# Which DMA queue carries the output stores: SyncE's or GpSimd's, in a fused attention and mixture kernel

## The chip, the cores and the metric

The kernel runs on one NeuronCore of a Trainium2 chip. The metric is the time of one execution on the device in microseconds (us). The core has TensorE (PE), VectorE (DVE), ScalarE (ACT), GpSimd (POOL) and SyncE (SP). Transfers between HBM and SBUF, the memory on the core, run on 16 DMA engines. An engine's sequencer issues a transfer to a queue. SyncE's transfers appear in the profile as queue q1 (hardware_dynamic), GpSimd's as queue q0 (software_dynamic). A transfer is moved as packets; the profile counts packets and bytes for each queue.

## The reference, cut to what matters

```python
# attention: q, k, v are (4, 8, 768, 64); half of the heads see all earlier keys,
# the others the first 4 keys and a window of 64
a = softmax(mask(q @ k.T / 8)); attn = a @ v
x = attn.transpose(0, 2, 1, 3).reshape(3072, 512)
# soft mixture of experts: 8 experts, 4 slots each, F = 1024
logits = x @ phi                                  # 3072 x 32
slot_input = softmax(logits, over rows).T @ x     # 32 x 512
slot_out[e] = relu(slot_input[e] @ w1[e]) @ w2[e] # 8 experts, 512 -> 1024 -> 512
out = softmax(logits, over slots) @ slot_out      # 3072 x 512, float32
```

The output is 3072 x 512 float32, 6.29 MB. It depends on all of `slot_out`, which depends on the last expert weight, so nothing can be stored before the end of the program.

## The kernel before, in words

The attention part works through 16 pairs of batch and heads and fills most of the time. During it GpSimd issues the loads of q, k, v and of the expert weights; its queue converts float32 in HBM to bf16 in SBUF on the way ("casting queue"). The loads follow each other on q0 without a pause. The order of all work is made at build time by a small planner (`Plan`): each piece of work (`pl.op`) has an engine, a key, costs and the work that it depends on; the planner places what can start earliest, the lower key first, and the instructions of each engine are emitted in that order.

The end of the program is what the change touches:

- The second weights of the last two experts are loaded in two column halves each (`load_half`), in the order 14.0, 15.0, 14.1, 15.1. With the first halves, columns 0 to 255 of `slot_out` can be finished (`SO.0`), with the second halves columns 256 to 511 (`SO.1`).
- The 3072 rows of the output are 6 row groups `gi` of 512 rows. Row 512 * gi + 4 * p + r lies on partition p, at place r (0 to 3). So one partition of a group holds 4 whole rows, 8 KB, one after another both in SBUF (`ot_view(gi)`) and in HBM.
- `out_tile` makes one tile (gi, r): a matmul on PE (line 1130) into a PSUM bank, then a scaled copy to SBUF on DVE (line 1140) or ACT (line 1138).
- Groups 0 to 2 (`NL = 12` tiles) are made in two halves: first the "l" tiles (left, columns 0 to 255, after `SO.0`), later the "r" tiles (right, columns 256 to 511, after `SO.1`). Groups 3 to 5 are made whole ("f" tiles, 512 columns).
- `store(eng, m, gi, r0, r1, cs, key)` (issue at line 1149) stores the places r0 to r1 - 1 of a group, columns `cs`, through GpSimd's queue if `eng` is "POOL", otherwise through SyncE's. It depends on the copies of just those tiles. A store of half rows has runs of 1 KB in HBM, which lie 2 KB apart; a store of whole rows has 8 KB on each partition in one piece. Nothing is converted in a store: SBUF and HBM are both float32.

The stores before: on GpSimd the left ones of group 0 (place 0: 128 KB; places 1 to 3: 384 KB); on SyncE the left ones of groups 1 and 2 in two of 256 KB each, the right ones of groups 0 to 2 in two of 256 KB each, and the whole rows of groups 3, 4 and 5, 1024 KB each. That is 2 stores on GpSimd and 13 on SyncE, which also issues three loads at the start. GpSimd has no other work in this part. At the program's end SyncE waits for every store to land, and all engines meet in barriers (line 1217).

Of the kernel before, what the change touches and what calls it, by code (L numbers as in the profile page):

```python
# [226 lines left out]
def kernel(  # L227
# [101 lines left out]
    def on(eng, occ, late=0.18):  # L329
        return {eng: (occ, occ + late)}  # L330
# [651 lines left out]
    kt = T * 16 + 10  # L982
# [137 lines left out]
    def ot_view(gi):  # L1120
        return slots[wbuf[gi].slot][:, 0:8 * KB].bitcast(F32).rearrange("p (r d) -> p r d", r=4)
# [3 lines left out]
    def out_tile(m, gi, r, c0, c1, key):  # L1125
        bf, w = Buf("BK"), 256 * (c1 - c0)
        cs = slice(256 * c0, 256 * c1)

        def emit_om(o):
            nc.tensor.matmul(banks[bf.slot][:, 0:w], out_lhs(gi, r), slot_out[:, cs], start=True, stop=True)  # L1130

        a = pl.op(f"OM.{gi}.{r}.{c0}", on("PE", 0.06 + w / 2400.0, 0.27), key, deps=so_e[c0:c1], acq=[bf],
                  emit=emit_om, mode="full", mm=1)

        def emit_oe(o):
            d, sc_ = ot_view(gi)[:, r, cs], rrow[:, 4 * gi + r:4 * gi + r + 1]
            if o.eng == "ACT":
                nc.scalar.activation(d, banks[bf.slot][:, 0:w], ACT.Copy, scale=sc_)  # L1138
            else:
                nc.vector.tensor_scalar(d, banks[bf.slot][:, 0:w], sc_, None, op0=ALU.mult)  # L1140

        x, y = (0.24 + w / 1070.0, 0.13 + w / 960.0)
        oe[m, gi, r] = pl.op(f"OE.{gi}.{r}.{c0}", {"ACT": (x, x + 0.19), "DVE": (y, y + 0.17)}, key, deps=[a, o_rw[gi]],
                             rel=[bf], emit=emit_oe)

    def store(eng, m, gi, r0, r1, cs, key):
        def emit_st(o):
            dst = out[512 * gi:512 * (gi + 1), :].rearrange("(p r) d -> p r d", r=4)
            (nc.gpsimd if eng == "POOL" else nc.sync).dma_start(dst[:, r0:r1, cs], ot_view(gi)[:, r0:r1, cs])

        pl.op(f"ST.{m}.{gi}.{r0}", on(eng, 0.7), key, deps=[oe[m, gi, r] for r in range(r0, r1)], emit=emit_st)

    NL = 12
    halved = [(gi, min(4, NL - 4 * gi)) for gi in range((NL + 3) // 4)]
    for gi, n in halved:
        for r in range(n):
            out_tile("l", gi, r, 0, 1, kt + 30 + 0.1 * (4 * gi + r))
    for gi, r0, r1 in [(0, 0, 1), (0, 1, 4)] + [(gi, x, x + 2) for gi, n in halved[1:] for x in (0, 2)]:
        store("SP" if gi else "POOL", "l", gi, r0, r1, slice(0, 256), kt + 31 + gi + 0.1 * r0)
    for gi, n in halved:  # L1160
        for r in range(n):
            out_tile("r", gi, r, 1, 2, kt + 40 + 0.1 * (4 * gi + r))
        for r0, r1 in [(0, 2), (2, 4)]:
            store("SP", "r", gi, r0, r1, slice(256, 512), kt + 41 + gi + 0.1 * r0)
    for gi in range(6):
        n = dict(halved).get(gi, 0)
        for r in range(n, 4):
            out_tile("f", gi, r, 0, 2, kt + 41 + 0.1 * (4 * gi + r))
        if n < 4:
            store("SP", "f", gi, n, 4, slice(0, 512), kt + 42 + gi)  # L1170

    pl.limit = kt - 0.2
    pl.tune(SHIFTS)
# [48 lines left out]
```

## Time and profile before

| what | value |
|---|---|
| median of 3 runs | 147.64 us (147.49 to 147.65) |
| the profiled execution | 147.56 us |
| its span, first to last instruction | 145.8 us |
| DMA packets, bytes | 14648, 33.40 MB |
| queue q0 (GpSimd) | 26.22 MB, 92.9% of 16 engines' span |
| queue q1 (SyncE) | 6.88 MB, 12.7% |
| busy share of PE, DVE, ACT, POOL | 85%, 76%, 74%, 28% |

The profile is one execution. Its windows give for a stretch the busy time of each engine with the number of instructions, the clock that was granted to PE, the mean share of the 16 DMA engines that were busy, and the rate in GB/s of what they moved (a load that converts is counted by the bytes that it writes). A share above 1 means that packets overlap on an engine. The DMA view of a stretch gives the packets, the bytes and the share of each queue, and for an issue the time until its data landed.

### The profile page before, as it was taken

The page shows a single profiled execution, that of the slowest core. Times are in us where ns is not written, and L with a number is a line of the kernel's source. Part 1 is how long each engine was busy: PE and PEld are TensorE (multiplying, and loading weights), DVE is VectorE, ACT ScalarE, POOL GpSimd, SP SyncE. Part 2 cuts the span into 40 slices and gives each one's busy share as a digit, 9 for nine tenths or more (in the row PEclk, how much of TensorE's full clock was granted, in tenths as well). Part 3 has the DMA queues.
Part 4 walks back from the last instruction along what each step waited for, and adds up shares of the span by engine and source line. Part 5 has one row for each costly group of instructions (what it writes and reads, how often), then busy time and mean ns, then how long its engine had stood idle before and what let it go on. Part 6 is the DMA issues. An engine that isn't in the chain of part 4 may idle for free.

```text
span 145.8 us, 4941 instructions
## 1 busy us (share of the span) xinstructions
PE 124.6 (85%) x2134; PEld 82.3 (56%) x2134; DVE 110.8 (76%) x254; ACT 107.9 (74%) x147; POOL 40.5 (28%) x73
## 2 busy tenths in 40 slices
PE   6959989999999999999989999999959899869100
PEld 4437566676776758776548766666737355444000
DVE  1796399999999999999799899999983312449700
ACT  3152799999999988999998999999971461549300
POOL 6988631310311470100170011405380000110000
PEclk9985699999999999999999999999995999999965
DMA  5999999999999999999999999999999999999995
GB/s 135 277 208 211 215 215 214 212 216 214 215 214 214 216 215 214 216 214 211 215 214 215 214 216 219 212 217 215 217 210 215 211 194 197 185 321 362 407 420 247
DMA packets 14648, 33.40 MB, mean 229 GB/s; under 512 B 867, under 2 KB 7651, under 8 KB 14115
## 3 DMA queue, kind: packets, MB, share of 16 engines
q0 software_dynamic: 11184, 26.22, 92.9%
q1 hardware_dynamic: 3442, 6.88, 12.7%
q8 instruction: 16, 0.26, 0.6%
q14 instruction: 6, 0.04, 0.1%
HBM read 52.49 MB, written 6.29 MB: 403 GB/s over the span
## 4 chain that ended last, share of the span: by engine, by line
PE 28%; DVE 25%; DMA 18%; ACT 15%; issue 6%; POOL 1%; SPq 0%; DVEq 0%; ACTq 0%; POOLq 0%
DMA qk<-in_moe_w_dram 15%; ACT pt L735 11%; PE sc L665 6%; DVE pt L681 5%; PE pv L809 5%; DVE xv L833 5%; DMA phf<-in_moe_phi_dram 4%; DVE qk L336 3%; PE tr L613 3%; PE tr L639 3%; PE bk L1130 3%; PE tr L872 2%; DVE slot L1140 2%; DVE vf L714 2%; PE tr L845 2%
## 5 line engine op out<-in xcount | busy, mean ns | idle before, releaser
L735 ACT ACTIVATE pt<-sc 128x1024 bf16<-128x1024 f32 x80 | 77.0, 1049 | 3.0 <-PE sc L665 2.8
L665 PE MATMUL sc<-qk 64*128 64x512 bf16 (+3 forms) x256 | 31.3, 311 | 1.2 <-ACT pt L735 0.8
L681 DVE TENSOR_TENSOR pt<-pt,msk 128x1024 bf16<-128x1024 bf16 (+1 forms) x48 | 29.0, 609 | 2.0 <-ACT pt L735 1.8
L809 PEld LDWEIGHTS <-pt 128*128 128x128 bf16 x640 | 23.7, 98 | 6.2 <-issue 5.2
L809 PE MATMUL pv<-vx,pt 128*128 128x65 bf16 x320 | 25.9, 194 | 0.3 <-DVE xv L833 0.2
L809 PE MATMUL pv<-vf,pt 128*128 128x65 bf16 x320 | 21.6, 196 | 0.9 <-DVE xv L833 0.9
L347 POOL DMA_DIRECT2D slot<-in_moe_w_dram x11 | 7.8, 705 | 39.3 <-PE tr L639 29.5
L639 PE MATMUL tr<-ident,slot 128*64 128x128 bf16 (+1 forms) x448 | 16.3, 219 | 0.4 <-ACT qk L334 0.3
L336 DVE COPY qk<-tr 128x768 bf16<-128x768 bf16 (+2 forms) x33 | 15.1, 481 | 1.5 <-PE tr L613 1.3
L639 PEld LDWEIGHTS <-slot 128*64 128x64 bf16 (+1 forms) x448 | 13.1, 109 | 5.1 <-issue 4.8
L833 DVE TENSOR_TENSOR xv<-pv,rs 128x768 bf16<-128x768 f32 (+1 forms) x17 | 15.5, 910 | 0.6
L665 PEld LDWEIGHTS <-qk 64*128 64x128 bf16 x256 | 10.4, 94 | 9.6 <-issue 3.3
L1140 DVE TENSOR_SCALAR slot<-bk,rrow 128x256 f32<-128x256 f32 (+1 forms) x19 | 9.2, 561 | 2.2 <-PE bk L1130 2.2
L896 POOL COPY expT<-eT 128x192 bf16<-128x192 bf16 x12 | 7.4, 657 | 12.2 <-ACT eT L879 12.2
L336 DVE COPY xv<-tr 128x512 bf16<-128x512 bf16 (+2 forms) x20 | 7.9, 409 | 2.4 <-PE tr L613 2.2
L845 PE MATMUL tr<-ident,xv 128*128 128x128 bf16 x96 | 8.4, 224 | 1.3 <-DVE xv L833 0.9
L613 PE MATMUL tr<-ident_u,slot 96*64 96x96 bf16 x192 | 7.3, 238 | 1.9 <-DVE phi L553 1.4
L613 PEld LDWEIGHTS <-slot 96*64 96x64 bf16 x192 | 6.3, 133 | 4.5 <-issue 4.1
L336 DVE COPY xT<-tr 128x768 bf16<-128x768 bf16 (+1 forms) x14 | 7.5, 538 | 1.1 <-PE tr L845 1.1
L1138 ACT ACTIVATE slot<-bk,rrow 128x256 f32<-128x256 f32 (+1 forms) x17 | 7.7, 569 | 0.9 <-PE bk L1130 0.9
L699 PE MATMUL tr<-ident,xv 128*128 128x128 bf16 x96 | 8.1, 220 | 0.0
L845 PEld LDWEIGHTS <-xv 128*128 128x128 bf16 x96 | 6.0, 99 | 2.9 <-DVE xv L833 1.7
(123 smaller groups left out, 169.0 us busy)
## 6 DMA issues: line engine op xcount, KB each, us to landing
slot<-in_moe_w_dram POOLq DMA_DIRECT2D x10, 1024.0 KB, 24.5
out_dram<-slot SPq DMA_DIRECT2D x3, 1024.0 KB, 6.2
out_dram<-slot SPq DMA_DIRECT2D x10, 256.0 KB, 3.2
slot<-in_q_dram POOLq DMA_DIRECT2D x2, 768.0 KB, 19.4
slot<-in_k_dram POOLq DMA_DIRECT2D x2, 768.0 KB, 24.1
qk<-in_moe_w_dram SPq DMA_DIRECT2D x1, 1024.0 KB, 6.1
slot<-in_v_dram POOLq DMA_DIRECT2D x2, 512.0 KB, 21.3
qk<-in_moe_w_dram POOLq DMA_DIRECT2D x1, 1024.0 KB, 17.5
```

What stands on the lines that cost most here:

```text
L336: nc.vector.tensor_copy(dst, src)
L347: acq=[buf] if buf else [], lead=1.3, emit=lambda o: nc.gpsimd.dma_start(dst(), src))
L613: nc.tensor.transpose(t[64 * i:64 * (i + 1), :, :, s, :], rv[:, i, 8 * c + s, :], ident_u)
L639: nc.tensor.transpose(t[64 * i:64 * (i + 1), :, s, :], rv[:, i, 8 * c + s, :], ident[0:R, 0:R])
L665: nc.tensor.matmul(scb[sc.slot][:, i, c:c + 128 * nb], kk, qq.rearrange("p b c -> p (b c)"), start=True, stop=True)
L681: nc.vector.tensor_tensor(pT, pT, mh, op=ALU.mult)
L699: nc.tensor.transpose(t[:, 128 * j:128 * (j + 1)], vT[:, 6 * n + j, :], ident)
L735: nc.scalar.activation(pTs[PTb[b, n].slot][:, :, 512 * g:512 * (g + 1)], scb[sc.slot], ACT.Exp, scale=scale)
L809: nc.tensor.matmul(pvb[:, bk, c:c + 65], lt, rhs, start=(j == 0), stop=(j == i))
L833: nc.vector.tensor_tensor(xo, pvw[:, :, :, 0:64], r.rearrange("p i (j o) -> p i j o", o=1).to_broadcast([P, 2, i1 - i0, 64]), op=ALU.mult)
L845: nc.tensor.transpose(t[:, 128 * i:128 * (i + 1)], xv[:, i, 128 * n:128 * (n + 1)], ident)
L1140: nc.vector.tensor_scalar(d, banks[bf.slot][:, 0:w], sc_, None, op0=ALU.mult)
```

## The change

All left stores go through GpSimd's queue, those of groups 1 and 2 in one transfer of 512 KB each. Of the right ones, the two of group 0 and the first of group 1 stay on SyncE (`4 * gi + r0 < 6`); the second of group 1 goes to GpSimd, and group 2 becomes one transfer of 512 KB there. Of the whole rows, group 3 goes to GpSimd; groups 4 and 5 stay on SyncE. Together with its three loads at the start, SyncE then issues eight transfers; GpSimd issues 7 stores instead of 2. The tiles and their order are as before.

```diff
-    for gi, r0, r1 in [(0, 0, 1), (0, 1, 4)] + [(gi, x, x + 2) for gi, n in halved[1:] for x in (0, 2)]:
-        store("SP" if gi else "POOL", "l", gi, r0, r1, slice(0, 256), kt + 31 + gi + 0.1 * r0)
+    for gi, r0, r1 in [(0, 0, 1), (0, 1, 4)] + [(gi, 0, n) for gi, n in halved[1:]]:
+        store("POOL", "l", gi, r0, r1, slice(0, 256), kt + 31 + gi + 0.1 * r0)
     for gi, n in halved:
         for r in range(n):
             out_tile("r", gi, r, 1, 2, kt + 40 + 0.1 * (4 * gi + r))
-        for r0, r1 in [(0, 2), (2, 4)]:
-            store("SP", "r", gi, r0, r1, slice(256, 512), kt + 41 + gi + 0.1 * r0)
+        for r0, r1 in [(0, 2), (2, 4)] if gi < 2 else [(0, n)]:
+            store("SP" if 4 * gi + r0 < 6 else "POOL", "r", gi, r0, r1, slice(256, 512), kt + 41 + gi + 0.1 * r0)
     for gi in range(6):
         n = dict(halved).get(gi, 0)
         for r in range(n, 4):
             out_tile("f", gi, r, 0, 2, kt + 41 + 0.1 * (4 * gi + r))
         if n < 4:
-            store("SP", "f", gi, n, 4, slice(0, 512), kt + 42 + gi)
+            store("SP" if gi > 3 else "POOL", "f", gi, n, 4, slice(0, 512), kt + 42 + gi)
```

## The prediction

> **What bounds the kernel now.** I read the page first (slices of the span), then the windows of the last 20 us, the DMA queues in narrow windows, and the timelines of GpSimd, SyncE, VectorE and ScalarE there.
>
> ```profile
> span 145.8 us, 4941 instructions
> DMA  5999999999999999999999999999999999999995
> ```
>
> The 16 DMA engines are at 90% or more in all slices but the first and the last. The stores are the end of that: the windows of the last 18 us show it against the engines.
>
> ```profile
> core 0: us, PE busy (x) PEld busy (x) DVE busy (x) ACT busy (x) POOL busy (x), PEclk, DMA share, GB/s
> 126.00:128.00 2.00, 1.94 (x20) 0.94 (x19) 2.00 (x6) 1.89 (x6) 1.12 (x2) 1.00 1.15 167
> 128.00:129.00 1.00, 0.52 (x6) 0.17 (x3) 0.44 (x2) 0.40 (x2) 0.22 (x1) 1.00 1.15 294
> 129.00:131.00 2.00, 1.35 (x26) 1.01 (x26) 0.49 (x2) 0.62 (x2) 0.00 (x0) 1.00 0.99 362
> 131.00:134.40 3.40, 3.37 (x19) 1.63 (x17) 3.40 (x9) 3.40 (x9) 0.00 (x0) 1.00 1.05 362
> 134.40:136.40 2.00, 0.86 (x3) 0.10 (x1) 2.00 (x4) 1.85 (x4) 0.00 (x0) 1.00 1.09 383
> 136.40:144.00 7.60, 0.00 (x0) 0.00 (x0) 1.13 (x2) 0.00 (x0) 0.00 (x0) 0.72 1.03 426
> ```
>
> The last two columns are the DMA share and rate. VectorE's last tile ends in the 136.4 window, yet transfers run on for 6 us at full share. From 129 on the share never falls below 0.99, so a tile that is ready earlier gains nothing; only bytes per microsecond count. And the rate is not constant: about 362 to 383 GB/s, then 426. The end hangs on the last store of SyncE:
>
> ```profile
> 137.60 0.36 SPq L1149 DMA_DIRECT2D out_dram<-slot  x1
> out_dram<-slot SPq DMA_DIRECT2D x1, 1024.0 KB, 7.3
> ```
>
> It lands at 137.60 + 7.3 = 144.9, and 0.9 us of closing barriers follow. The profiled execution took 147.56 us, 1.8 more than its span; the median of the runs is 147.64. I work from 147.56.
>
> Why the rate differs is seen in the DMA queues of three windows: 131.2 to 136.4 (only half-row stores on SyncE's queue, q1), 129.6 to 130.4 (GpSimd's 384 KB left store on q0, beside a little of q1), 138 to 143 (whole rows on q1).
>
> ```profile
> DMA packets 1991, 1.92 MB, mean 369 GB/s; under 512 B 119, under 2 KB 1991, under 8 KB 1991
> q1 hardware_dynamic: 1991, 1.92, 106.5%
> ...
> DMA packets 129, 0.32 MB, mean 406 GB/s; under 512 B 7, under 2 KB 64, under 8 KB 129
> q0 software_dynamic: 65, 0.27, 86.6%
> q1 hardware_dynamic: 64, 0.06, 20.8%
> ...
> DMA packets 292, 2.13 MB, mean 426 GB/s; under 512 B 32, under 2 KB 32, under 8 KB 32
> q1 hardware_dynamic: 292, 2.13, 101.3%
> ```
>
> A half row is 1 KB of HBM. SyncE's queue makes a packet of each (1.92 MB in 1991 packets); GpSimd's queue puts several in one (0.27 MB in 65 packets: 4 KB each), although the runs in memory are the same. Engine time per MB is share x 16 x window / MB: 1.065 x 16 x 5.2 / 1.92 = 46.1 for 1 KB packets, 0.866 x 16 x 0.8 / 0.27 = 41.1 for 4 KB, 1.013 x 16 x 5 / 2.13 = 38.1 for 8 KB.
>
> **The change part by part.** *What moves.* Left stores of row groups 1 and 2 (four of 256 KB become two of 512 KB), the second right store of group 1 (256 KB), the right ones of group 2 (two become one of 512 KB): 7 x 262144 B = 1.835 MB of half rows go from q1 to q0, that is from 1 KB to 4 KB packets. So does the first whole-row store (group 3, 1.049 MB), which has 8 KB packets already. SyncE keeps three right stores of 256 KB and two whole-row ones.
>
> *Packing.* 1.835 MB take 4.97 us at 369 GB/s and 4.52 at 406: 0.45 us gained. Bounds: at 426, the rate of 8 KB packets, 0.67 gained; at 358, which is the rate of a microsecond in which both queues were busy,
>
> ```profile
> DMA packets 222, 0.36 MB, mean 358 GB/s; under 512 B 22, under 2 KB 172, under 8 KB 222
> q0 software_dynamic: 59, 0.21, 55.5%
> q1 hardware_dynamic: 163, 0.15, 43.4%
> ```
>
> (129 to 130) it is 5.13, 0.15 lost. I take 406, because 0.27 of that window's 0.32 MB is just this kind of packet. [...]
>
> *The start.* The first left stores stand behind the last weight piece on q0. Before, SyncE's queue fills engines that are through with weights.
>
> ```profile
> 126.78 0.57 POOL L1149 DMA_DIRECT2D out_dram<-slot  x1 [17.83 <-DVE slot L1140]
> 127.46 0.76 POOL L1149 DMA_DIRECT2D out_dram<-slot  x1
> 127.35 2.03 SPq L1149 DMA_DIRECT2D out_dram<-slot  x4
> ...
> DMA packets 58, 0.03 MB, mean 99 GB/s; under 512 B 0, under 2 KB 58, under 8 KB 58
> DMA packets 29, 0.04 MB, mean 399 GB/s; under 512 B 0, under 2 KB 22, under 8 KB 29
> ...
> DMA packets 118, 0.09 MB, mean 299 GB/s; under 512 B 8, under 2 KB 116, under 8 KB 118
> q1 hardware_dynamic: 51, 0.05, 49.2%
> ```
>
> The windows are 127.6 to 127.9, 127.9 to 128.0 and 128.3 to 128.6. No 4 KB packet runs in the first, seven start in the second: GpSimd's first store needs 1.15 us from issue to first packet, so its second (127.46) runs from 128.6. SyncE's needs 0.95 (127.35 to 128.3). Between 128.3 and 128.6 q1 moved 0.05 MB that now has no carrier: 0.05 / 0.38 = 0.13 us lost. Bounds: 0 if the weights' remainder speeds up by as much, 0.26 if a second such stretch is lost.
>
> *The whole-row store on q0.* If q0 cuts it into 4 KB, 1.049 MB go from 426 to 406 GB/s: 0.12 lost; if it stays at 8 KB, 0. I take 0.06.
>
> *Issues and waits.* SyncE drops 8 of 13 issues, GpSimd gets 5 more of 0.57 to 0.76 us; it is idle (0.00 busy) after its second. Larger stores wait for four tiles instead of two. The queued bytes hide both, as long as they last, so I followed the supply. Left: the second store is through at about 129.6; the third is issued at 127.46 + 0.76 = 128.2 and has packets at 129.4, the fourth at about 130.2. After 128.6 there are 1.573 - 0.131 = 1.44 MB of left stores and by my estimate the time of 0.1 MB for the last weight packets; 1.54 / 0.406 = 3.8 us, to 132.4. The first right store:
>
> ```profile
> 129.46 0.40 PE L1055 MATMUL bk<-qk,xT 128*32 128x256 bf16 x8 [0.95 <-DMA qk<-in_moe_w_dram]
> 131.39 0.37 SPq L1149 DMA_DIRECT2D out_dram<-slot  x1
> 132.99 0.66 SPq L1149 DMA_DIRECT2D out_dram<-slot  x1
> 133.10 1.14 DVE L1140 TENSOR_SCALAR slot<-bk,rrow 128x256 f32<-128x256 f32 x2
> 135.12 0.57 SPq L1149 DMA_DIRECT2D out_dram<-slot  x1
> ```
>
> 131.39 + 0.95 = 132.35, in time by nothing; q1's left stores no longer run beside the last weight piece, whose landing starts this chain (129.46), so it may come 0.1 to 0.4 earlier. What packing gains on the left beyond that is lost as a gap. Right: SyncE's three need 0.786 / 0.369 = 2.1 us, to 134.5; GpSimd's first can be issued at 132.99 (packets 134.15), its second at about 133.6, when VectorE turns from half tiles to whole ones (134.75); both are through at 136.5. The whole-row store, issued by 135.12, has packets at 136.3. So no gap, with 0.2 us to spare. Sum: -0.45 + 0.13 + 0.06 = -0.26; 147.56 - 0.26 = 147.30.
>
> **The rivals.** *Packing saves nothing* where other traffic sets the pace. For: packets on q1 overlap (share 106.5%), so their price is less than engine time says, and the windows 129 to 131 show 362 with half of the bytes on q0. Against: 406 at 129.6 to 130.4. Then the start and the whole-row store remain: +0.13 + 0.06 = +0.19, 147.75. [...]
>
> *Slower: two queues beside each other cost the engines.* Before, both hold stores only from 128.3 to 131. Now they do from 134 on: 0.79 MB of half rows and 1.05 MB of whole rows on q0, against 0.3 and some 1.1 MB on q1. At the rates of one queue alone, 1.1 / 0.369 + 2.15 / 0.426 = 8.0 us for 3.25 MB; at the 358 of 129 to 130, 9.1. Against it -0.26 of the left part (1.049 MB) and +0.13 of the start: +0.9, 148.5. It decides from 398 GB/s down (8.03 + 0.13 us), and from 384 the kernel is slower by over 0.2%. Against: in 129 to 130 some engines were still short of stores (share 0.99, not 1.06).
>
> *Slower: GpSimd's drain ends last.*
>
> ```profile
> out_dram<-slot POOLq DMA_DIRECT2D x1, 384.0 KB, 4.1
> L1217 POOLq DRAIN  x3: 51/98/5717, 127.4 to 145.5; - x3
> ```
>
> Its first drain ran from 127.4 to 133.1, 1.6 us after its last store landed (127.46 + 4.1 = 131.5). If that follows the landing, a whole-row store on q0 that lands after 144.9 - 1.6 = 143.3 moves the end; landing with SyncE's last, by 1.6 - 0.26: 148.9. It is queued 2 us ahead of SyncE's last, so I hold this unlikely.
>
> **How the numbers follow.** About 0.2%, 0.3 us, is what a measurement of this kernel can tell from no change. The forecast, packing gains net between -0.7 and -0.1 us: 0.54, of which I give 0.42 to the part beyond 0.2% of the median (under 147.34). Nothing saved: 0.12. Two queues cost: 0.28, of which 0.04 stays within 0.2%. The drain: 0.06. So faster 0.42, same 0.12 + 0.12 + 0.04 = 0.28, slower 0.24 + 0.06 = 0.30. The likeliest is 147.3. The range goes from 146.9 (packing at its upper bound, -0.67, and a start that costs 0) to 148.2, most of the way to the second rival; the likeliest case alone has 147.0 to 147.5.
>
> **What would show it.** q0 gains 2.88 MB (26.22 to 29.1), q1 falls to 4.0. Right: about 400 GB/s in 129.5 to 132 with 4 KB packets on q0, share 1.0 or more to the end, and SyncE's last store landing at 144.6. Wrong: windows under 398 GB/s after 134 with both queues in them (the second rival), a DMA share under 0.95 around 132.4 or 136.4 (stores run out before tiles), more than 0.2 us lost before 129, or GpSimd's drain as the last to end.

## Result and profile after

The changed kernel took 148.25 us (median of 7 runs, 147.99 to 148.54) beside 147.65 us for the kernel before (7 runs, 147.49 to 147.79) on the same chip: ratio 1.0039, 95% interval 1.0025 to 1.0052. It is slower by 0.6 us, where 147.3 had been forecast. (All ratios here leave out executions in which the chip was disturbed, so they can differ a little from the quotient of medians.) The profiled execution took 148.25 us.

Of the page after, the span, the DMA slices and the queues:

```profile
span 146.5 us, 4933 instructions
DMA  4999999999999999999999999999999999999995
GB/s 132 285 210 211 214 215 216 214 215 216 210 214 216 214 213 215 215 214 215 214 214 214 215 215 215 215 216 215 215 215 215 207 195 198 178 337 346 376 418 242
q0 software_dynamic: 11840, 29.10, 97.6%
q1 hardware_dynamic: 1394, 4.00, 7.2%
```

The bytes moved as the change says: 29.10 MB on q0, 4.00 on q1. The slices of the span are too coarse to show the loss. The windows of the last 18 us, cut as those of the kernel before were (DMA share and GB/s are the last two columns):

```profile
126.00:128.00 2.00, 2.00 (x10) 1.19 (x8) 2.00 (x6) 2.00 (x5) 1.30 (x2) 0.50 1.08 168
128.00:129.00 1.00, 1.00 (x11) 0.25 (x10) 0.40 (x1) 0.60 (x2) 0.82 (x3) 0.76 0.96 219
129.00:131.00 2.00, 1.40 (x26) 1.05 (x26) 0.42 (x2) 0.56 (x2) 0.67 (x1) 1.00 0.97 359
131.00:134.40 3.40, 3.37 (x19) 1.63 (x18) 3.40 (x9) 3.40 (x8) 0.93 (x2) 1.00 1.00 352
134.40:136.40 2.00, 0.93 (x4) 0.15 (x2) 2.00 (x4) 1.92 (x4) 1.08 (x2) 1.00 0.94 337
136.40:144.00 7.60, 0.00 (x0) 0.00 (x0) 1.20 (x2) 0.00 (x0) 0.00 (x0) 0.65 1.01 411
```

Against before the rate is 294 to 219 in the window from 128, 362 to 359, 362 to 352, 383 to 337 and 426 to 411. Rate times length gives 0.08, 0.01, 0.03, 0.09 and 0.11 MB less, 0.32 MB in all; at 420 GB/s that is 0.76 us, and the span grew by 0.7. From 128 on no stretch is faster. The clock that was granted to TensorE was lower in this execution (0.50 in 126 to 128, 1.00 before), but the loss at the start is not its doing: the trace of e1 (below), with 1.00 there, has 232 GB/s in 128 to 129. Two things can lower a rate: engines that stand idle (share below 1) and packets that take longer (share at 1, low rate). Both are there, in the trace after:

```profile
129.60:130.00 0.40, 0.40 (x13) 0.19 (x13) 0.00 (x0) 0.02 (x1) 0.07 (x1) 1.00 0.79 287
134.80:135.20 0.40, 0.33 (x2) 0.00 (x0) 0.40 (x2) 0.40 (x2) 0.13 (x1) 1.00 0.86 310
135.60:136.00 0.40, 0.00 (x0) 0.00 (x0) 0.40 (x2) 0.40 (x2) 0.40 (x1) 1.00 0.66 236
137.20:137.60 0.40, 0.00 (x0) 0.00 (x0) 0.40 (x1) 0.00 (x0) 0.00 (x0) 1.00 0.92 338
```

In these four the engines ran dry; what is missing to a share of 1 is (0.21 + 0.14 + 0.34 + 0.08) x 0.4 = 0.31 us. The trace before has one such dip, too (0.85, 290 GB/s in 128.8 to 129.2), worth 0.06 us, so the change added 0.25 to 0.31 by this estimate. The timelines of GpSimd and SyncE tell whose stores were late:

```profile
126.57 3.10 POOL L1149 DMA_DIRECT2D out_dram<-slot  x4 [19.41 <-DVE slot L1140]
133.41 1.51 POOL L1149 DMA_DIRECT2D out_dram<-slot  x2 [3.74 <-DVE slot L1140]
135.53 0.55 POOL L1149 DMA_DIRECT2D out_dram<-slot  x1 [0.60 <-ACT slot L1138]
...
131.47 6.54 SPq L1149 DMA_DIRECT2D out_dram<-slot  x5
```

GpSimd issued its right stores from 133.41 and the whole-row one at 135.53; SyncE had issued the same two at 132.99 and 135.12 before. Longer packets show in the DMA queues of two windows in which q0 alone was at work, 130 to 131.2 (left store of group 1) and 131.6 to 132.8 (left store of group 2):

```profile
DMA packets 121, 0.47 MB, mean 389 GB/s; under 512 B 7, under 2 KB 7, under 8 KB 121
q0 software_dynamic: 121, 0.47, 99.6%
...
DMA packets 103, 0.40 MB, mean 336 GB/s; under 512 B 3, under 2 KB 5, under 8 KB 103
q0 software_dynamic: 101, 0.40, 95.6%
```

Both are packets of 4 KB on the same queue. Engine time per MB, worked out as in the prediction, is 0.996 x 16 x 1.2 / 0.47 = 40.7 for group 1, but 0.956 x 16 x 1.2 / 0.40 = 45.9 for group 2, about the 46.1 of 1 KB packets before.

### The profile page after: what moved, and what is told of

It reads as the page before. It is cut to its first block, busy times and chain, and to the rows that moved or that the text cites. A ratio compares the mean times of both kernels' runs of the same rounds, so it can differ in the third digit from the quotient of the medians.

```text
span 146.5 us, 4933 instructions
## 1 busy us (share of the span) xinstructions
PE 121.8 (83%) x2134; PEld 80.7 (55%) x2134; DVE 111.5 (76%) x254; ACT 108.3 (74%) x147; POOL 43.8 (30%) x78
## 3 DMA queue, kind: packets, MB, share of 16 engines
q0 software_dynamic: 11840, 29.10, 97.6%
## 4 chain that ended last, share of the span: by engine, by line
DVE 31%; PE 30%; DMA 16%; ACT 7%; issue 5%; POOL 3%; DVEq 0%; POOLq 0%; ACTq 0%
DMA qk<-in_moe_w_dram 16%; PE sc L665 7%; PE pv L809 7%; DVE pt L681 6%; DVE xv L833 5%; DVE qk L336 4%; ACT pt L735 4%; PE tr L639 4%; DVE xv L336 3%; PE bk L1130 3%; DVE vf L714 2%; PE tr L845 2%; PE tr L613 2%; PE tr L872 2%; DVE vx L336 2%
## 5 line engine op out<-in xcount | busy, mean ns | idle before, releaser
L1149 POOL DMA_DIRECT2D out_dram<-slot x7 | 4.8, 686 | 24.1 <-DVE slot L1140 23.2
L1130 PE MATMUL bk<-msk,expT 128*128 128x256 bf16 (+1 forms) x36 | 7.5, 355 | 0.9 <-ACT msk L1113 0.8
L613 PE MATMUL tr<-ident_u,slot 96*64 96x96 bf16 x192 | 5.8, 207 | 2.0 <-DVE phi L553 1.2
```

What stands on the lines that cost most here:

```text
L613: nc.tensor.transpose(t[64 * i:64 * (i + 1), :, :, s, :], rv[:, i, 8 * c + s, :], ident_u)
```

## Experiments

Theories, by the letters that the expectations use. A: GpSimd's stores come late and the engines run dry. B: 4 KB packets are no cheaper than 1 KB ones while VectorE and ScalarE write SBUF. C: two queues beside each other cost the engines. D: the rate falls with what is left in a queue. E: the rate depends on the place, that is on the address in SBUF where a group's data starts.

**The parts alone.** Each takes one part of the change and leaves the rest as before.

```diff
 e1_left_only    left, groups 1 and 2:  SP 4 x 256 KB  -> POOL 2 x 512 KB
 e2_right_only   right: group 1 second half -> POOL; group 2: SP 2 x 256 KB -> POOL 512 KB
 e3_whole_only   whole rows of group 3: SP -> POOL
```

> Only the left stores are as in the changed kernel (all on GpSimd, groups 1 and 2 in one transfer each); right and whole ones as before. Theory A (supply: GpSimd's stores reach the DMA engines later, so the engines run dry at the handovers): the start (0.06 MB less by 129.6 in the changed kernel's trace, 0.16 us) and the dip at 129.6 (294 GB/s, 0.05 us) stay, less some 0.05 us for 4 KB packets from 130 to 131: +0.1 to +0.2 us. Theory B (4 KB packets are not cheaper while VectorE and ScalarE write SBUF): the left part then loses only the start, +0.15. Prediction's view (packing gains 0.26 of the left part, start loses 0.13): -0.1. A and B are told apart in the trace: A wants dips in the rate, B packets of the same rate as 1 KB ones from 131.2 to 132.8.

> Only the right stores are as in the changed kernel (second of group 1 and all of group 2 on GpSimd); left and whole ones as before. Theory A: dips where SyncE's three right stores are through before GpSimd's first has packets (266 GB/s at 134.8 in the changed kernel) and before its second (291 at 135.6): +0.15 to +0.2 us. Theory B: 0.786 MB at about 345 instead of 383 GB/s: another +0.2 us, together +0.4. Prediction's view: -0.2 from packing.

> Only the whole rows of group 3 go through GpSimd's queue, all other stores as before. Theory A: SyncE's right stores keep the engines busy to about 136.9; GpSimd issues at about 135.5 and its packets come at about 137.0, so 0 to +0.15 us. Theory C (two queues beside each other cost the engines): 2.1 MB moved with both queues at work, at 358 instead of 426 GB/s up to +0.9 us; the changed kernel's trace at 427 GB/s there speaks for 0.

Measured: left alone 1.0013 [1.0001, 1.0025], right alone 1.0042 [1.0025, 1.0059], whole rows alone 1.0014 [0.9997, 1.0031]. No part gains. The right part costs most, and its own trace shows where:

```profile
134.40:134.80 0.40, 0.33 (x2) 0.00 (x0) 0.40 (x2) 0.40 (x2) 0.15 (x1) 1.00 0.84 312
134.80:135.20 0.40, 0.23 (x1) 0.00 (x0) 0.40 (x2) 0.40 (x2) 0.00 (x0) 1.00 1.08 415
135.20:135.60 0.40, 0.00 (x0) 0.00 (x0) 0.40 (x2) 0.40 (x2) 0.00 (x0) 1.00 0.64 236
```

Two dips, at the start of each of GpSimd's two stores. Counted as above they are worth 0.2 us, so they are a part of this run's loss and not all of it; group 2's slow packets are in it as well. The three parts add up to +0.69%, more than the whole change's 0.39%; their intervals are as wide as that difference.

**Waits and issues.** Is it the wait for four tiles instead of two, or GpSimd?

```diff
 e4_left_pairs   as e1, but the left stores in 256 KB pairs on POOL
 e13_merged_sp   512 KB stores for left 1, left 2 and right 2, all on SP
 e12_r2_pool     before, only the right store of group 2 on POOL (512 KB)
```

> As e1_left_only, but groups 1 and 2 on GpSimd in two transfers of 256 KB each, so each waits for two tiles instead of four. If waiting for four tiles is what loses time on the left, this is 0.1 us or more faster than e1_left_only. Theory A puts the loss on GpSimd's issue and first-packet time: GpSimd takes 0.6 to 0.75 us for each issue, 0.262 MB in 0.65 us is 400 GB/s, just what the engines take, so it is the same as e1_left_only or up to 0.2 us slower.

> The kernel before with the transfers merged as in the changed kernel (left of groups 1 and 2 and right of group 2 in one transfer of 512 KB each), all on the queues of before (SyncE). If waiting for four tiles is what costs, it is slower, on the left by about 0.1 us and more on the right. Theory A puts the cost on GpSimd's later packets (0.3 to 0.5 us to start, 1.15 us or more to the first packet) and expects no change within 0.2%.

> The kernel before with one change alone: the right stores of group 2 as one transfer of 512 KB on GpSimd's queue. SyncE then has four right stores, to about 135.3, and GpSimd's one has packets at about 135.4. Theory A (dry engines): the dip at 134.4 of e2_right_only (277 GB/s) is gone and the one at 135.2 to 135.6 shrinks: +0.05 to +0.2 us against the kernel before, at most half of the 0.42% that e2_right_only cost. If the price of 4 KB packets were the cause instead, two thirds of the bytes moved would cost two thirds of it: +0.4 us.

Pairs on GpSimd took 1.0043 [1.0026, 1.0059], more than e1; the merged stores on SyncE 0.9998 [0.9980, 1.0016]. So waiting for four tiles costs nothing that shows, and cutting the store on GpSimd makes it worse; that it has six issues in a row instead of four is the likely reason, but no run isolates it. With only the last right store on GpSimd, while SyncE's stores still fill the engines, the cost is 1.0013 [0.9993, 1.0033], and the dip is a slice at 0.93:

```profile
135.20:135.60 0.40, 0.24 (x1) 0.00 (x0) 0.40 (x2) 0.40 (x2) 0.00 (x0) 1.00 1.08 384
135.60:136.00 0.40, 0.00 (x0) 0.00 (x0) 0.40 (x2) 0.40 (x2) 0.00 (x0) 1.00 0.93 338
```

The trace bears A out, for the dips. The times do not decide: the interval is wide, and the medians, 148.14 and 147.73, are 0.4 us apart, which is what the price of 4 KB packets was expected to give.

**Packet size alone, with a full queue.** Groups 4 and 5 are stored as four half-row stores of 512 KB at the very end, where everything is ready: on SyncE (1 KB packets) or on GpSimd (4 KB).

```diff
-store("SP", "f", gi, 0, 4, slice(0, 512))                       # gi = 4, 5
+store(eng, "f", gi, 0, 4, slice(0, 256)); store(eng, "f", gi, 0, 4, slice(256, 512))
 e5_halves_sp: eng = SP      e6_halves_pool: eng = POOL
 e7, e8: the same two, with 16 extra copies on DVE and ACT meanwhile
```

> The kernel before, but the whole rows of groups 4 and 5 are stored as a left and a right half each (4 transfers of 512 KB, runs of 1 KB) on SyncE's queue. They run after about 139.4, when no engine computes. 1 KB packets at 384 GB/s: 2.097 MB in 5.46 us instead of 4.92 at 426, +0.54 us. This is the base for the next kernel, which has the same halves on GpSimd's queue.

> The same four halves on GpSimd's queue, so 4 KB packets while nothing computes, with 1 MB of group 3 queued ahead so that the queue can't run dry. Theory B (4 KB packets pay only while VectorE and ScalarE are quiet): 159 ns a packet, about 408 GB/s, 5.14 us: 0.3 us less than e5_halves_sp. If packing pays nothing at all: the same as e5_halves_sp. If it pays as the prediction took it (406): 0.3 us less too, so this run alone does not tell the prediction's rate from theory B; the busy pair does.

> As e5_halves_sp, with 8 more copies of 128x512 from PSUM to an unused part of SBUF on VectorE and on ScalarE each, after the last tile (to about 143.4). They feed nothing and the program does not wait for them beyond its usual end. Theory B: 1 KB packets on SyncE's queue keep 46 ns and 355 to 385 GB/s, so 0 to +0.4 us against e5_halves_sp.

> As e6_halves_pool, with the same added copies. Theory B: the 4 KB packets go from 159 to about 187 ns, 340 to 350 GB/s until 143.4, so about 0.6 us more than e6_halves_pool, and as slow as or slower than e7_halves_sp_busy. If the copies have nothing to do with it: packets of 159 ns and the time of e6_halves_pool.

e5 took 1.0063 [1.0045, 1.0082], e6 1.0193 [1.0153, 1.0232]: 4 KB packets lost to 1 KB ones by 1.9 us. The trace shows three causes. One is the drain, from the rows of line 1219 in e6's trace:

```profile
L1219 POOLq DRAIN  x3: 51/102/8967, 138.8 to 148.2; - x3
out_dram<-slot POOLq DMA_DIRECT2D x3, 512.0 KB, 5.7
```

GpSimd's drain began at 138.8 and took 8.97 us, to 147.7, 1.8 us after its last store landed (145.9 in the trace). There the drain was the end of the program. The second is a dip before GpSimd's first packets of group 4 (share 0.82, 303 GB/s in 139 to 140). The third is the rate: in e6 group 4 went at 365 to 385 GB/s (140 to 143), group 5 at 348 (143 to 145). In e7 (1.0311 [1.0238, 1.0384]) and e8 (1.0277 [1.0228, 1.0325]) the added copies read one PSUM bank, waited for each other (in e7 VectorE's for ScalarE's 5.3 us in all) and ran past the stores (in e7 to 148.9, with 5 GB/s moved from 145 on), so their times say nothing; but 1 KB packets ran at 385 (140 to 143) and 4 KB ones at 385 (140 to 142) and then 348 beside them, much as without. B falls.

**Order or place.** Group 5 was last in the queue in e6. In e9 it goes first; in e10 a whole-row store is queued behind e5's halves.

```diff
 e9_halves_pool_swapped:      POOL order 4, 4, 5, 5 -> 5, 5, 4, 4
 e10_halves_sp_then_whole:    SP order 3, 4, 4, 5, 5 -> 4, 4, 5, 5, 3 (3 whole, 1024 KB)
```

> As e6_halves_pool, but the halves of group 5 go first and those of group 4 last. In e6_halves_pool the first two transfers moved at 360 to 410 GB/s and the last two at 347. Theory D (what is queued behind a transfer sets its rate: the last ones of a queue are slow): again the first two at 360 to 410, the last two (now group 4) at about 347. Theory E (the place of the data sets it): group 5, now first, at 347 and group 4, now last, at 360 to 410.

> As e5_halves_sp, but group 3's whole rows (8 KB packets) are stored last on SyncE's queue, behind the four halves. In e5_halves_sp the last half went at 345 to 365 GB/s, the others at 385. Theory D: with 1 MB queued behind it, the last half goes at 385 too. If it is the place of the data, the right half of group 5 stays at 350.

One execution each, 150.83 and 149.26 us. The DMA queues of e9 in 142 to 143.2 (group 5, now first) and 144 to 145 (group 4, now last):

```profile
DMA packets 103, 0.40 MB, mean 331 GB/s; under 512 B 6, under 2 KB 6, under 8 KB 103
q0 software_dynamic: 103, 0.40, 100.0%
...
DMA packets 116, 0.41 MB, mean 410 GB/s; under 512 B 16, under 2 KB 16, under 8 KB 116
q0 software_dynamic: 116, 0.41, 100.3%
```

The slow rate went with group 5, not with the end of the queue; in e10 its right half, in 1 KB packets, stayed at 348 (141.4 to 142.4) with 1 MB behind it. D falls, E stands. What differs between the groups is where their slots start in SBUF: the six groups begin 64, 0, 128, 128, 0 and 192 B past a multiple of 256 B (slots of 8256 B follow each other). Groups 1 and 4, at 0, are the fast ones (389 GB/s in the changed kernel, 365 to 410 in e6 and e9); 2 and 5, at 128 and 192, are slow (336 in the changed kernel, 331 to 348 in e6 and e9); group 0, at 64, gave a mixture (before, 406 in 4 KB packets and, from 132 to 134, 355 in 1 KB ones). Both fast groups start on a multiple of 256 B and neither slow one does; whether that sets the rate is the next test.

**Start addresses.** The same tiles in another order in SBUF, so that all six groups start on a multiple of 256 B, or (groups 1 and 4 put in other places) none does.

```diff
-slots = [sb.tile([P, 8 * KB + 2 * PAD], BF16, name=f"slot{i}") for i in range(11)]
+slots = [None] * 11
+for i in (0, 1, 4, 3, 2, 6, 5, 7, 8, 9, 10):                    # not aligned
+    slots[i] = sb.tile([P, 8 * KB + 2 * PAD], BF16, name=f"slot{i}")
+# aligned: order 0, 4, 5, 7, 1, 9, 2, 10, 3, 6, 8, with small tiles ahead of some of them
 e14 / e15 / e16 / e19 aligned: before / after / e6 / e12
 e17 / e18 not aligned:         before / after
```

> The kernel before with its SBUF tiles laid out anew: the tiles from which the six row groups are stored start at multiples of 256 B. In the kernels so far the start of groups 0 to 5 is 64, 0, 128, 128, 0 and 192 B past a multiple of 256, and 4 KB packets moved at 380 to 420 GB/s from groups 1 and 4 and at about 345 from groups 2 and 5. Theory E (the start of the data in SBUF sets the rate): the stretch of 1 KB packets from 131.6 to 134.4 (groups 2 and 0 on SyncE's queue, 355 GB/s) goes at about 385: 0.2 us less, and the rest as before: -0.1 to -0.3 us. If compute or the number of queued transfers set that stretch: no change.

> The changed kernel with the same new layout. Theory E: group 2's left and right transfers, 4 KB packets at 342 to 361 and 343 GB/s, go at 400 or more: 1.05 MB in 2.6 instead of 3.0 us, 0.4 us less where the engines do not run dry instead; dips stay. So 0.2 to 0.5 us less than the changed kernel, about the time of the kernel before, 147.7 to 148.0; against e14_before_aligned 0.1 to 0.5 us slower by the dry engines (theory A). If the place is nothing: 148.25.

> e6_halves_pool with the same new layout. Theory E: all four halves at 400 GB/s or more, those of group 5 too (347 in e6_halves_pool, and 330 in e9_halves_pool_swapped), so 0.4 to 0.6 us less than e6_halves_pool. If it is the place in HBM that counts: group 5 stays at about 347.

> The kernel before with two pairs of SBUF tiles exchanged in the layout, so that groups 1 and 4, which started at a multiple of 256 B, now start 192 and 128 B past one, like the others. Nothing else moves. Theory E: the 1 KB packets of group 1 on SyncE's queue (385 GB/s) can fall to 350: 0.79 MB, up to +0.2 us; 1 KB packets of groups 2 and 5 were seen at both rates, so 0 to +0.2 us.

> The changed kernel with the same exchange. Theory E: the last 4 KB packets that were fast, group 1's left transfer (390 to 410 GB/s) and its right one, go at 345 as well: 0.79 MB in 2.3 instead of 1.95 us, +0.2 to +0.4 us against the changed kernel, 148.5 to 148.7; against e17_before_misaligned +0.5 us or more, more than the 0.4% of the change as it is. If the alignment were nothing: 148.25.

> e12_r2_pool (only group 2's right store on GpSimd's queue) in the layout of e14_before_aligned. With all starts aligned its 4 KB packets go at 410 against 385 GB/s: 0.52 MB, 0.1 us gained where the engines do not run dry before it (0.1 us in e12_r2_pool): the time of e14_before_aligned within 0.1 us, so 147.5 to 147.8, and less than e12_r2_pool by 0.1 to 0.4 us.

Ratios are to the kernel before as it was:

| SBUF layout | order before | order after |
|---|---|---|
| as it was | 1 | 1.0039 [1.0025, 1.0052] |
| all aligned | e14: 0.9985 [0.9966, 1.0003] | e15: 0.9994 [0.9973, 1.0014] |
| none aligned | e17: 1.0016 [0.9999, 1.0032] | e18: 1.0074 [1.0045, 1.0103] |

The DMA queues in stretches with one queue at work: 4 KB packets in e15 (130 to 131.6) and e18 (131.2 to 132.8); 1 KB packets in e14 and e17 (132.8 to 136 in both).

```profile
DMA packets 181, 0.66 MB, mean 412 GB/s; under 512 B 20, under 2 KB 20, under 8 KB 181
q0 software_dynamic: 181, 0.66, 102.4%
```

```profile
DMA packets 151, 0.55 MB, mean 346 GB/s; under 512 B 16, under 2 KB 16, under 8 KB 151
q0 software_dynamic: 151, 0.55, 101.2%
```

```profile
DMA packets 1271, 1.23 MB, mean 383 GB/s; under 512 B 74, under 2 KB 1271, under 8 KB 1271
q1 hardware_dynamic: 1271, 1.23, 108.9%
```

```profile
DMA packets 1154, 1.11 MB, mean 348 GB/s; under 512 B 67, under 2 KB 1154, under 8 KB 1154
q1 hardware_dynamic: 1154, 1.11, 103.6%
```

Aligned, 4 KB packets beat 1 KB ones by 412 to 383; not aligned, both run at about 347 and packing saves nothing. Group 5's halves on GpSimd, 348 in e6, ran at 410 when aligned, with the same places in HBM (e16, 142 to 144; its time was 1.0108 [1.0063, 1.0154], down from 1.0193):

```profile
DMA packets 218, 0.82 MB, mean 410 GB/s; under 512 B 18, under 2 KB 18, under 8 KB 218
q0 software_dynamic: 218, 0.82, 102.1%
```

The address is not all, though: group 4, aligned in all of these runs, went at 365 to 389 when it was first on GpSimd's queue (e6, e16) and at 410 when it was last (e9, 144 to 145). That stays open. So does a part of e18's time: 148.5 to 148.7 us had been expected, 149.04 was measured, and its six executions go from 148.21 at a mean granted clock of TensorE of 0.96 to 149.40 at 0.92. What the address does is read from the rates above, at full share.

The dips do not go away: e15's four are deeper than those of the changed kernel.

```profile
132.00:132.40 0.40, 0.40 (x3) 0.30 (x2) 0.40 (x2) 0.40 (x3) 0.00 (x0) 0.50 0.60 228
134.40:134.80 0.40, 0.40 (x3) 0.19 (x2) 0.40 (x1) 0.23 (x2) 0.40 (x1) 0.81 0.74 292
135.20:135.60 0.40, 0.40 (x4) 0.17 (x2) 0.40 (x2) 0.38 (x2) 0.12 (x1) 1.00 0.46 184
136.80:137.20 0.40, 0.00 (x0) 0.00 (x0) 0.40 (x2) 0.34 (x1) 0.00 (x0) 1.00 0.85 348
```

(The first of them falls where e14, too, waits for tiles, and the clock in the first two was 0.50 and 0.81, so not all of their depth is GpSimd's.) So in the aligned layout packing about pays for the late stores and no more: e15 can't be told from e14. e19, aligned, with only the last right store on GpSimd, had the lowest median of all, 147.52, at 0.9991 [0.9975, 1.0006]. Neither it nor e14 can be told from the kernel before. In e14 the aligned transfers outrun the tiles (share 0.68 in 131.6 to 132.4, 1.07 before), which is where their gain can go.

## Why the prediction was wrong

*Packing* is the step that was mis-sized most. It priced all 1.835 MB at 406 GB/s, the rate of one 0.8 us window with group 0's store, and gained 0.45 us. In the changed kernel the two 512 KB stores of group 2 (1.05 MB) ran at about 345, slower than the 369 that they replaced: +0.2 us. The other 0.79 MB, from group 1, ran at 389 (left) and 399 (right, 135.2 to 135.6): -0.13 us. An estimate from these rates makes the term about +0.1 instead of -0.45. The bound on that side, 358 GB/s, was still too fast for more than half of the bytes. The start addresses set this, as e15 against e18 shows; how they do it inside an engine no run shows. The spread of the rates with 1 KB packets, 355 to 385 in the trace before, had been averaged to 369.

*Issues and waits* failed too: "no gap, with 0.2 us to spare". It took over SyncE's issue times. GpSimd's wait for the second right store of group 1 ended at 132.90 in the trace, and the issue came at 133.41; for the whole-row store 135.0 and 135.53, 0.5 us later each time, where SyncE needed less than 0.1 (132.96 to 132.99 before). The next issue then stood behind the first (134.19 instead of 133.6). The first packets of the store of 133.41 came at 135.12, 1.7 us after its issue instead of 1.15. The engines ran dry for up to 0.31 us in all. Of the two places that the prediction had named for this, the share fell to 0.66 just before 136; around 132.4 it stayed at 0.96, and the packets were slow instead (group 2's). Nor did the first right store come 0.1 to 0.4 us earlier (131.47 against 131.39).

*The start* was right: 0.075 MB less in 128 to 129, 0.18 us at 420 GB/s, for +0.13 with a bound of 0.26. *The whole-row store on q0* keeps its packets of 8 KB (0.87 MB in 106 packets on q0 from 138 to 142), so the +0.06 falls away; what e3 lost, not clear of zero, stands around the store's first packets (337 GB/s in 136 to 137, share 0.78 in 137.2 to 137.6).

Sum, as an estimate: 0.1 + 0.18 + 0.25 to 0.31 = +0.5 to +0.6, against +0.6 in the medians and +0.7 in the profiled spans.

The rivals. *Packing saves nothing* (147.75) was nearest by its mechanism, though the reason, the address, was not in it; it left out the gaps. *Two queues beside each other* fell: from 138 to 142 both held whole rows, and the trace after shows

```profile
138.00:142.00 4.00, 0.00 (x0) 0.00 (x0) 0.00 (x0) 0.00 (x0) 0.00 (x0) 0.59 1.01 424
```

424 GB/s, as fast as one queue. The sign that the prediction had set for it, under 398 GB/s after 134, did show (337 in 134.4 to 136.4), but from idle engines, as the shares of 0.86 and 0.66 tell. *The drain* did not decide: in the changed kernel it began at 135.50 and took 9.445 us, to 144.9,

```profile
L1217 POOLq DRAIN  x3: 51/98/9445, 135.5 to 146.2; - x3
```

1.8 us after the whole-row store landed (143.1), while SyncE's last store landed at 145.6. Its mechanism is real: in e6 it was the end.

## What to carry to other kernels

Before a transfer is moved to another queue for larger packets, look up in SBUF where its data starts: here the same 4 KB packet ran at 412 or at 346 GB/s, and a rate read from one group's store did not hold for the next group's (389 for group 1's left one, 336 for group 2's). Follow the supply with the issue times of the engine that will issue, not of the one that did: here half a microsecond more before an issue left DMA engines idle (share 0.66 at the worst). GpSimd's last store should land well ahead of the last store of all, because its drain ended up to 1.8 us after it.

## What was not expected of the hardware

- Start address in SBUF: 4 KB packets 412 GB/s aligned to 256 B and 346 not, 1 KB packets 383 and 348, so 19% and 10%. Why is not shown: no trace tells what an engine does inside a packet. For 1 KB packets the start does not decide alone: in the layout as it was, some stores from unaligned groups ran at 384 to 385 (right half of group 2 before, left half of group 5 in e5) and others at 348 to 355 (right half of group 5 in e10, group 0 before). That stays open.
- GpSimd began an issue 0.3 to 0.5 us after the wait for its tiles was satisfied (126.48 to 126.78 before, 132.90 to 133.41 and 135.00 to 135.53 after), SyncE after less than 0.1 us (131.36 to 131.39 before, 131.43 to 131.47 after).
- GpSimd's closing drain ended 1.6 to 1.8 us after its last store had landed (133.1 against 131.5 before, 144.9 against 143.1 after, 147.7 against 145.9 in e6).
